# Half of a weight quarter by SyncE's queue in FP32, with a cast on VectorE

## The chip, the core and the metric

The kernel runs on one core of one Trainium2 chip. The metric is the device time of one execution in microseconds (us); the span of a profile is the time from the first to the last instruction of the program inside that execution. The engines go by the profile's names: PE is TensorE (PEld its weight loads), DVE is VectorE, ACT is ScalarE, POOL is GpSimd and SP is SyncE.

## The reference

Attention over 8 batches of 8 heads, 576 tokens and 64 columns per head, with a causal window of 128 tokens and a slope per head on the distance; then a layer norm over the 512 columns of a token and a two-layer perceptron of width 2048, added to its input:

```python
scores = scale * np.matmul(q, k.transpose(0, 1, 3, 2))
mask = (rel >= 0) & (rel < window)
scores = np.where(mask, scores + bias[None], -1000000000.0)
attn = np.exp(scores - np.max(scores, axis=-1, keepdims=True))
x = np.matmul(attn / attn.sum(axis=-1, keepdims=True), v)   # then (B, S, H * D)
xn = (x - mu) / np.sqrt(var + 1e-06) * g_ln
ch = np.maximum(xn @ w_ch1, 0.0) @ w_ch2
return (x + ch).astype(np.float32)
```

All inputs are FP32 in DRAM. The kernel's matmuls take FP16.

## The kernel before, in words

**Tiling.** The 8 x 576 tokens are cut into 36 blocks of 128 tokens (`order`: four pairs of batches, nine blocks each; the ninth holds the 64 last tokens of both batches). A block goes through scores (L500), exponentials on ACT (L511), a mask on DVE (L533), values (L596), the row sums and their reciprocal (L604, L605), and centring (L633, L637). Then it is transposed into `xT` and goes through the perceptron with a group of blocks: the first four groups have two blocks, the other seven have four.

**The weights.** `w1` is the first weight matrix as a tile of 128 partitions x `NKB` = 4 row blocks (`kb`) x 2048 columns in FP16. A quarter of it, c0 to c3, is 512 columns of all four row blocks: 1 MB in DRAM, 512 KB in SBUF. The matmuls of L870 take the 128 columns of one `fb` and go through the four `kb`; c0 serves `fb` 0 to 3, c1 `fb` 4 to 7, and so on. `w1g` is `w1` times the layer norm's gain; `gain_w1` (L226) makes it on DVE from 30 us on. Until then `w1g` is unused. The first two groups use `w1` and have the gain in `xT` (L664, L669, from `g_sb`).

**The loads.** POOL issues nearly all of them, since its queue converts FP32 to FP16 on the way. Their order is the list `loads`: the four loads of `first` (L192: queries and keys of the first block, of batch 0 and then batch 1), values of blocks 0 and 1 (L291), queries and keys of the next blocks (L256, two loads each), c0 of `w1` (L217), values of blocks 2 and 3, c1, c2 and c3 of `w1`, then `w2` by quarters (L236) and further queries, keys and values. POOL's loads have eight semaphores, taken in turn, so the ninth load is issued when the first has landed. SP carries two small loads at the start, the tables (L1288) and the gain `g_sb` (L1289), and next an output at 46 us.

**The order of the work.** Every engine's order is written out by hand: `steps` is a list of groups of calls, and `weave_at` puts them between the matmuls of the perceptron. The steps around the change are these.

- `warm_step(n)`: n matmuls on a tile of ones (L336), which nothing reads.
- `slopes` (L204, DVE, from the tables) and `decay` (L161, ACT); then `add_distances` (L465, PE).
- `turn_first(0)`: the first block of batch 0 is transposed on PE (L416) and copied out of PSUM, queries by DVE (L421) and keys by ACT (L422). Scores follow. The same for batch 1.
- values and centring of those two blocks, `x_step` 0 and 1 (`xT`), the next blocks' queries and keys (`turn_second`, L348, and `copy_second`, L441) and their scores.
- From here on, `mlp1_pair` runs: group 0's `fb` 0 to 11, group 1's `fb` 0 to 7, group 0's 12 to 15, group 1's 8 to 15. Between its first units stand the scores, masks and values of blocks 2 and 3, their transposes (L657) and the steps after them.

Of the kernel before, what the change touches and what calls it, by code (L numbers as in the profile page):

```python
# [11 lines left out]
FP32 = mybir.dt.float32  # L12
# [85 lines left out]
def kernel(  # L98
# [10 lines left out]
    nc = tc.nc  # L109
# [3 lines left out]
    NKB = DM // P  # L113
# [6 lines left out]
    def pool(name, bufs, **kw):  # L120
# [24 lines left out]
    ps_sc = [  # L145
        ps_scores.tile([P, 2, 4 * P], FP32, name=f"ps_sc{i}", tag=f"ps_sc{i}")
        for i in range(2)
    ]
# [24 lines left out]
    w1 = consts.tile([P, NKB, FFN], FP16)  # L173
    w1g = consts.tile([P, NKB, FFN], FP16)
# [37 lines left out]
    w1r = moe_w_ch1.rearrange("(kb p) f -> p kb f", p=P)  # L212
    w2r = moe_w_ch2.rearrange("(fb p) d -> p fb d", p=P)
    W1C = FFN // 4

    def load_w1(c):
        nc.gpsimd.dma_start(  # L217
            out=w1[:, :, c * W1C : (c + 1) * W1C], in_=w1r[:, :, c * W1C : (c + 1) * W1C]
        )

    def gain_w1(first, n):

# [73 lines left out]

    order = [(p, blk) for p in range(NPAIR) for blk in range(NSLOT)]
    w1s, w2s = ([(f, c) for c in range(4)] for f in (load_w1, load_w2))
    weights = {3: w1s[1:] + w2s[:2], 4: w2s[2:], 5: [(load_tables,)]}
    loads, place = [], []  # L300
# [18 lines left out]
    def load_until(n):  # L319
        nonlocal issued  # L320
        while issued < min(n, len(loads)):
            f, *args = loads[issued]
            f(*args)
            issued += 1
# [406 lines left out]
    def scores_step(n):  # L731
        return [(scores,) + order[n]]
# [19 lines left out]
    def warm_step(n):  # L752
        return [[(warm, n)]]
# [1 line left out]

    (low2, high2), (low3, high3) = ([[(attend, *args)] for args in attends(*order[n])] for n in (2, 3))
    steps = warm_step(5) + [[(slopes,), (decay, m_full)]]
    steps += [[(add_distances, ps_sc[b]) for b in range(2)]] + warm_step(1)
    steps += [[(turn_first, 0)], *warm_step(2), scores_step(0)] + warm_step(2)
    steps += [[(turn_first, 1)], *warm_step(2), scores_step(1)]  # L760
    steps += [[(values_at_once, 0, 0, 0), (centre, 0, 0)]] + warm_step(3)
# [27 lines left out]
    for n in range(8, ONE_GO):  # L789
# [14 lines left out]
        for tag, m in (("q", n + 5), ("k", n + 6)):  # L804
            if m < count and order[m][1] % 2 == 0 and by_dma(*order[m]):
                p, blk = order[m]
# [8 lines left out]
    for n in range(ONE_GO, count):  # L815
# [12 lines left out]
        for tag, m in (("q", n + 5), ("k", n + 6)):  # L828
            if m < count and order[m][1] % 2 == 0:
                p, blk = order[m]  # L830
# [455 lines left out]

    def start():
        nc.sync.dma_start(out=first_tables, in_=tables_dram[:, 0 : 3 * P])  # L1288
        nc.sync.dma_start(out=g_sb, in_=moe_g_ln.rearrange("(kb p) -> p kb", p=P))  # L1289
        load_until(place[7])  # L1290

# [6 lines left out]
    with tc.manual_schedule(engines={engine.PE}):  # L1298
        with tc.manual_schedule(engines={engine.Activation, engine.DVE, engine.SP, engine.Pool}):
            start()  # L1300
            advance_to(first)
            weave_at(mlp1_pair((0, 12), (0, 8), (12, NFB), (8, NFB)), 1, 2, 3, 3, 5, 7, 8, 18, 24, 28)
# [60 lines left out]
```

## Time and profile before

| what | before |
| --- | --- |
| time, median of 3 runs | 306.91 us (303.88 to 308.73) |
| the profiled execution: time | 304.83 us |
| its span | 303.1 us |
| granted TensorE clock, mean | 0.998 |
| PE busy | 292.4 us (96%) |
| DVE busy | 232.9 us (77%) |
| ACT busy | 184.6 us (61%) |
| POOL busy | 113.4 us (37%) |
| software DMA queue (POOL's) | 103792 packets, 18.46 MB |
| hardware DMA queue | 45840 packets, 18.60 MB |

The last row counts outputs and transposes besides the two small loads. "Busy" of PE counts pipelined matmuls with modelled ends. A DMA share above 1 in a window means that packets overlap on a DMA engine; the GB/s beside it are of bytes written.

### The profile page before, as it was taken

What the parts mean: (1) busy time and instruction counts of PE and PEld (TensorE: products, weight loads), DVE (VectorE), ACT (ScalarE), POOL (GpSimd) and SP (SyncE); (2) the same over time, 40 slices, a digit from 0 to 9 for tenths busy, and PEclk for the clock granted to TensorE, in tenths of its full rate; (3) what the DMA queues carried; (4) which work ended last, traced back from release to release, by engine and by line L of the source; (5) the groups of instructions that cost most, each with busy time, mean ns of one, the idle gap of its engine ahead of it and who ended that gap; (6) DMA issues with size and microseconds to landing.
All of it is one profiled execution on the core that took longest, in us unless ns stands there. A gap on an engine that the chain in (4) does not pass through costs nothing.

```text
span 303.1 us, 9275 instructions
## 1 busy us (share of the span) xinstructions
PE 292.4 (96%) x3783; PEld 201.0 (66%) x3783; DVE 232.9 (77%) x617; ACT 184.6 (61%) x338; POOL 113.4 (37%) x153
## 2 busy tenths in 40 slices
PE   7679999999999999999999999999999999999994
PEld 2368755866755578656865686568656865788883
DVE  3578678789996788658866886687788878878983
ACT  6578777868967883478457745674577456506500
POOL 8843659683882571684007171760000000000000
PEclk9999999999999999999999999999999999999999
DMA  9999999999999999999979999999561143006014
GB/s 97 170 200 202 193 160 149 202 136 114 147 138 159 171 157 146 148 197 141 123 125 145 151 104 158 139 135 130 108 123 35 21 98 77 19 17 141 3 35 104
DMA packets 150234, 38.03 MB, mean 125 GB/s; under 512 B 140688, under 2 KB 146080, under 8 KB 150192
## 3 DMA queue, kind: packets, MB, share of 16 engines
q0 software_dynamic: 103792, 18.46, 82.7%
q1 hardware_dynamic: 45840, 18.60, 38.8%
q8 instruction: 29, 0.48, 0.7%
q10 hardware_dynamic: 560, 0.39, 0.5%
q14 instruction: 13, 0.11, 0.1%
HBM read 36.90 MB, written 9.44 MB: 153 GB/s over the span
## 4 chain that ended last, share of the span: by engine, by line
PE 88%; DMA 5%; DVE 2%; POOL 1%; ACT 1%; issue 1%; DVEq 0%; POOLq 0%
PE ps_m L870 36%; PE ps_s L1100 22%; PE ps_m L900 9%; PE ps_sc L500 5%; PE ps_sc L596 4%; PE ps_q L1178 4%; DMA w<-in_moe_w_ch_dram 3%; PE ps_x L994 3%; DMA vx<-in_v_dram 2%; POOL first L192 1%; DVE probs L533 1%; PE ps_tx L657 1%; PE ps_pv L567 1%; PE ps_tr L348 1%; PE ps_t L994 1%
## 5 line engine op out<-in xcount | busy, mean ns | idle before, releaser
L870 PE MATMUL ps_m<-xT,w1g 128*128 128x512 f16 (+1 forms) x512 | 104.0, 353 | 0.1
L886 ACT ACTIVATE ht_all<-ps_m 128x512 f16<-128x512 f32 (+1 forms) x143 | 72.0, 511 | 38.6 <-PE ps_m L870 36.6
L870 PEld LDWEIGHTS <-w1g 128*128 128x128 f16 x512 | 47.7, 98 | 41.5 <-issue 0.3
L511 ACT ACTIVATE probs<-ps_sc 128x1024 f16<-128x1024 f32 x56 | 56.1, 1022 | 9.1 <-PE ps_sc L500 9.1
L291 POOL DMA_DIRECT2D vx<-in_v_dram x40 | 35.0, 888 | 67.6 <-PE ps_sc L596 51.5
L1100 PE MATMUL ps_s<-w,s 128*128 128x256 f16 x384 | 45.7, 273 | 0.0
L1100 PEld LDWEIGHTS <-s 128*128 128x128 f16 x384 | 36.8, 98 | 4.3 <-issue 0.2
L533 DVE TENSOR_TENSOR probs<-probs,m 128x1024 f16<-128x1024 f16 x56 | 36.2, 684 | 1.7 <-ACT probs L511 1.7
L1100 PE MATMUL ps_s<-w,ht_all 128*128 128x256 f16 x288 | 36.1, 273 | 0.0
L681 ACT ACTIVATE junk<-xc 128x512 f16<-128x512 f16 x28 | 17.7, 631 | 26.8 <-DVE xc L637 26.8
L900 PE MATMUL ps_m<-w,ht_all 128*128 128x512 f16 x128 | 31.5, 380 | 0.0
L1100 PEld LDWEIGHTS <-ht_all 128*128 128x128 f16 x288 | 27.4, 98 | 4.9
L920 DVE TENSOR_TENSOR s<-ht_all 128x1024 f16<-128x1024 f16 (+2 forms) x36 | 20.5, 569 | 11.3 <-ACT ht_all L886 10.4
L280 POOL DMA_DIRECT2D q<-in_q_dram x40 | 27.6, 711 | 3.1 <-DMA vx<-in_v_dram 1.8
L500 PEld LDWEIGHTS <-k 64*64 64x64 f16 x1088 | 15.5, 107 | 13.5 <-issue 11.6
L605 DVE SCALAR_TENSOR_TENSOR x<-ps_sc,rec 128x512 f16<-128x512 f32 x32 | 22.1, 692 | 1.2 <-DVE rec L604 0.2
L1121 DVE SCALAR_TENSOR_TENSOR o<-ps_s,rstd,x 128x256 f32<-128x256 f32 x48 | 20.9, 477 | 2.6 <-PE ps_s L1100 2.2
L500 PE MATMUL ps_sc<-q,k 64*64 64x128 f16 (+1 forms) x1088 | 21.1, 211 | 1.2 <-ACT k L422 0.6
L277 POOL DMA_DIRECT2D k<-in_k_dram x20 | 17.9, 913 | 6.2 <-DMA k<-k 5.3
L604 DVE RECIPROCAL rec<-ps_sc 128x8 f32<-128x8 f32 x32 | 6.5, 204 | 16.4 <-PE ps_sc L596 16.3
L596 PEld LDWEIGHTS <-probs 128*128 128x128 f16 x384 | 15.9, 98 | 3.6
L900 PEld LDWEIGHTS <-ht_all 128*128 128x128 f16 x128 | 11.0, 98 | 10.6
(116 smaller groups left out, 374.2 us busy)
## 6 DMA issues: line engine op xcount, KB each, us to landing
out_dram<-o SPq DMA_DIRECT2D x64, 128.0 KB, 3.0
vx<-in_v_dram POOLq DMA_DIRECT2D x32, 128.0 KB, 6.6
w<-in_moe_w_ch_dram POOLq DMA_DIRECT2D x8, 512.0 KB, 11.4
k<-in_k_dram POOLq DMA_DIRECT2D x30, 128.0 KB, 7.2
q<-in_q_dram POOLq DMA_DIRECT2D x48, 64.0 KB, 5.8
q<-in_q_dram POOLq DMA_DIRECT2D x10, 128.0 KB, 7.8
out_dram<-o SPq DMA_DIRECT2D x9, 64.0 KB, 2.0
k<-in_k_dram POOLq DMA_DIRECT2D x8, 64.0 KB, 6.5
```

The costliest lines, as they stand in the source:

```text
L280: nc.gpsimd.dma_start(out=t[half, b], in_=tokens.rearrange("h (c r) d -> r c h d", r=2)[r],)
L291: nc.gpsimd.dma_start(out=vx[p0 : p0 + n, :, 0:D], in_=v[b, :, t0 : t0 + n, :].rearrange("h p d -> p h d"),)
L500: nc.tensor.matmul(in_halves(ps[cols, j, n, t, :])[:, r, queries], kt[rows, hp, cols], in_halves(qt[rows, b, hp])[:, r, queries], start=no ...
L511: nc.scalar.activation(out=dst.rearrange("p (n j) q -> p j n q", j=2), in_=ps.rearrange("p j n t q -> p j n (t q)"), func=AF.Exp, scale=in ...
L533: nc.vector.tensor_tensor(out=dst, in0=dst, in1=mask, op=ALU.mult)
L596: nc.tensor.matmul(ps[:, h, 0 : D + 1], pr[:, h, t, :], vext[(p * NSLOT + o) % NV][:, h, :], start=(n == 0), stop=(n == len(terms) - 1),)
L605: nc.vector.scalar_tensor_tensor(out=x.rearrange("p (h d) -> p h d", h=H), in0=ps[:, :, 0:D], scalar=1.0, in1=rec.unsqueeze(2).broadcast_t ...
L870: nc.tensor.matmul(ps[:, 0:cols], w[:, kb, fb * P : (fb + 1) * P], xT[:, kb, 0:cols], start=(kb == 0), stop=(kb == NKB - 1),)
L886: nc.scalar.activation(out=ht[:, fb, :], in_=ps[:, 0:cols], func=AF.Relu)
L900: nc.tensor.matmul(sums[at], ht[:, fb, at * P : (at + 1) * P], w2[:, fb, :], start=(fb == 0), stop=(fb == NFB - 1),)
L1100: nc.tensor.matmul(ps[:, pair, :], lhs[:, fb, at : at + P], rhs[:, fb, :], start=(first and pair == 0 and fb == 0), stop=(fb == half - 1), ...
L1121: nc.vector.scalar_tensor_tensor(out=outs[at][:, cols], in0=ps[:, pair], scalar=rstd[:, n : n + 1], in1=(xs[p, blk] if fresh else outs[at] ...
```

## The change

Of quarter c0, row blocks 0 and 1 no longer come by POOL's queue. SP issues their load, as plain FP32, between its two loads at the start; 512 KB go to the place of `w1g`'s first row block, seen as FP32. DVE casts them into `w1`, in an instruction that stands after `slopes` and before the first copy of `turn_first(0)`. POOL's load of c0 keeps row blocks 2 and 3, at its old place in the order.

```diff
+    by_sync, first_half = slice(0, NKB // 2), w1g[:, 0].bitcast(FP32)
+    first_half = first_half.rearrange("p (kb f) -> p kb f", kb=NKB // 2)
+
     def load_w1(c):
-        nc.gpsimd.dma_start(
-            out=w1[:, :, c * W1C : (c + 1) * W1C], in_=w1r[:, :, c * W1C : (c + 1) * W1C]
-        )
+        kbs, cols = slice(by_sync.stop if c == 0 else 0, NKB), slice(c * W1C, (c + 1) * W1C)
+        nc.gpsimd.dma_start(out=w1[:, kbs, cols], in_=w1r[:, kbs, cols])
+
+    def cast_first_half():
+        nc.vector.tensor_copy(out=w1[:, by_sync, 0:W1C], in_=first_half)
...
-    steps += [[(add_distances, ps_sc[b]) for b in range(2)]] + warm_step(1)
+    steps += [[(add_distances, ps_sc[b]) for b in range(2)] + [(cast_first_half,)]] + warm_step(1)
...
     def start():
         nc.sync.dma_start(out=first_tables, in_=tables_dram[:, 0 : 3 * P])
+        nc.sync.dma_start(out=first_half, in_=w1r[:, by_sync, 0:W1C])
         nc.sync.dma_start(out=g_sb, in_=moe_g_ln.rearrange("(kb p) -> p kb", p=P))
```

## The prediction

> **What bounds the kernel now.** I read the chain of waits first, restricted to the first 24 us, since the change touches nothing later. Its columns are start, length (us) and what was done.
>
> ```profile
> 4.92 6.44 DMA vx<-in_v_dram
> 11.37 0.28 issue
> 11.65 9.84 DMA w<-in_moe_w_ch_dram
> 21.49 0.05 issue
> 21.53 1.05 PE ps_m L870 x8
> ```
>
> The start is bound by the queue of loads: a load of values lands at 11.37, a load of w1 at 21.49, and PE takes up L870 at 21.53. From there to the end the chain is nearly all PE (88% of the whole span), so what is won or lost by about 25 us is carried to the end. Next the waits of PE in the same stretch (us in total, times, longest):
>
> ```profile
> PE ps_tr L348 <- DMA k<-in_k_dram: 1.3, 1, 1.3
> PE ps_m L870 <- DMA w<-in_moe_w_ch_dram: 0.9, 1, 0.9
> PE ps_sc L596 <- DMA vx<-in_v_dram: 0.5, 1, 0.5
> PE ps_tr L416 <- DMA first<-in_k_dram: 0.3, 1, 0.3
> ```
>
> All waits of PE for loads come to 3.0 us; nothing in the change can win more than that. The timeline says where they are (start, length, engine, line, operation, tiles, shape, count, idle time before it):
>
> ```profile
> 3.63 0.49 DVE L204 TENSOR_SCALAR ht_all<-first_tables 128x128 f16<-128x128 f16 x1
> 6.40 0.42 DVE L421 COPY q<-ps_tr 128x512 f16<-128x512 f16 x1 [2.28 <-PE ps_tr L416]
> ...
> 15.32 0.44 PE L348 MATMUL ps_tr<-first_tables,k 64*64 64x64 f16 x30 [1.27 <-DMA k<-in_k_dram]
> 17.27 0.77 PEld L870 LDWEIGHTS <-w 128*128 128x128 f16 x8 [0.23 <-DMA w<-in_moe_w_ch_dram]
> 21.48 0.69 DVE L533 TENSOR_TENSOR probs<-probs,m 128x1024 f16<-128x1024 f16 x1
> 21.53 1.05 PE L870 MATMUL ps_m<-xT,w 128*128 128x256 f16 x8 [0.95 <-DMA w<-in_moe_w_ch_dram]
> 22.42 0.65 PE L596 MATMUL ps_sc<-vx,probs 128*128 128x65 f16 x16
> 24.68 0.23 PEld L657 LDWEIGHTS <-xc 128*128 128x128 f16 x4 [0.29 <-DVE xc L637]
> ```
>
> L870 begins when c0 is there (17.27), but that wait is hardly one: the scores before it end at 16.57 + 0.64 = 17.21, by their own row of the timeline. The real stall is the 0.95 us before 21.53, for c1. So the change is worth something only by letting c1 land earlier in the same queue.
>
> Last, how full the DMA engines are (window and length, busy time of PE, PEld, DVE, ACT, POOL, clock, DMA share, GB/s written):
>
> ```profile
> 2.00:3.00 1.00, 1.00 (x4) 0.38 (x3) 0.22 (x3) 0.23 (x2) 1.00 (x3) 1.00 0.52 84
> 3.00:6.00 3.00, 2.75 (x17) 0.80 (x19) 1.12 (x7) 2.34 (x8) 3.00 (x5) 1.00 1.32 126
> 6.00:9.00 3.00, 2.68 (x84) 1.25 (x84) 0.76 (x2) 2.04 (x3) 3.00 (x5) 1.00 1.97 148
> ```
>
> They are half empty from 2 to 3 us, at 1.32 from 3 to 6, and at 1.97 when fullest.
>
> **What c1 gains.** Queries and keys of the second block release PE at 15.32, c0 at 17.27; the two are neighbours in the queue, so c0 takes 1.95 us of it. Half of it is 0.98 us, and c1 would land at 21.49 - 0.98 = 20.51. PE's matmuls before the stall end at 21.53 - 0.95 = 20.58, so the stall goes. The quarters behind c1 come earlier by as much.
>
> **Where that stall goes.** PE doesn't get all of the 0.95 us. After the eight matmuls of L870 (8 x 0.11 = 0.88) PE wants the values of block 3 (L596) at about 21.5 instead of 22.42. The second half of their weights is masked by the L533 that runs on DVE from 21.48 to 22.17, and this stands behind DVE's work on block 2, which has nothing to do with c1. So the last eight of the sixteen matmuls start at 22.17 at the earliest, and L596, with 0.33 to 0.45 us for them, ends at about 22.6 instead of 23.07. The reciprocal, x, mean and centring of block 3 follow on DVE, and the transposes at 24.68, which wait for that centring, come 0.45 us earlier. So the gain is 0.45 us with nothing on the other side.
>
> **What the new load costs.** It moves 512 KB as 2 KB rows, 256 of them, through the same 16 DMA engines. No load of this kind is in the trace. The nearest row is w1's and w2's own quarters: two POOL loads that wait for successive quarters are issued at 26.84 and 29.38, thus 2.54 us for 512 rows of 2 KB read, and 1.27 us for 256. Upper bound: the whole 1.27 us is taken from POOL's queue, everything up to the keys at 15.32 comes later by that, and c1 lands 1.27 - 0.98 = 0.29 later. Lower bound: nothing, because the new packets find idle engines. SP's tables take 2.0 us from issue to landing (0.74 to 2.74), so the half, issued at 1.1, should flow from about 2.2; from 2 to 3 us there is 1.4 of 1.97 in share to spare, and from 3 to 6 there is 0.65 x 3 = 1.95. That is more than its need, but the first packets of queries and keys lie in the same microseconds, and their landing paces what follows. I take 0.3, near the lower bound, for the part that meets the queue after 3 us.
>
> A rule of the Trainium skill stands against this choice: DMA: Bandwidth & Descriptors, "Issuing engines are not separate DMA queues", says that transfers started by different engines run on the same 16 DMA engines, and that spreading them saves only issue time. By it the term is the upper bound, 1.27; the share of 0.52 beside 1.97 says that the engines are not full when this load comes.
>
> **The cast.** DVE is idle from 4.12 (the end of L204) to 6.40. Landing of the half: at the earliest 1.1 + 2.0 + 1.27 = 4.4, at the latest, with half of the engines' time, 1.1 + 3.0 (an output of 128 KB by SP takes that) + 2.54 = 6.6; I take 5.0. The cast itself, 1024 FP32 elements per partition, isn't in the trace: below, twice the 284 ns of the fastest row (L1043, 512 FP16 elements in SBUF), 0.57; above, twice L878's 683 ns from FP32, 1.37; I take 0.7, as L533 with 1024 elements. While POOL prepares loads, DVE's short instructions stretch: L204 takes from 175 to 495 ns, so 0.3 more. It ends at about 6.0, inside the gap, and costs nothing. Queued behind it are the copies L421, for which the scores wait. If it landed at 6.6 and took 1.37, L421 would end at 8.4 instead of 6.82, and the scores of the first block would begin at 8.4 instead of 7.22; PE's 0.5 us wait for values and its 1.27 us wait for keys at 15.32 take up 1.2 of it, nearly all. So the cover is wide; without it the cost would be that 1.2.
>
> The Trainium skill warns of the cast too: SBUF — State Buffer, "SBUF: two separate sides", says that an FP32 copy of SBUF on VectorE locks GpSimd out of a shared port, so that it can't write descriptors. The stretched L204 agrees that the two meet. POOL would lose one cast; its values issued at 4.92 land at 11.37, far behind their issue, so the sum stays.
>
> **The smaller parts.** `g_sb`, moved behind the half in SP's queue, landed at 1.16 + 2.8 = 3.96 and is first used at 12.39 (L669); even 3 us later costs nothing, and its cover is those 8 us. SP issues nothing else before 46 us. POOL's c0 load has half the rows and needs no longer than before. DVE's writing of `w1g` begins at 30 us, long after the cast.
>
> **The sum.** The gain of 0.45 less 0.3 makes 0.15 us: a span of 303.1 - 0.15 = 302.95 and, with the 1.73 us around it, 304.7 against the profiled execution's 304.83. That execution lies 2.1 below the median of the runs shown; on the median, 306.91 - 0.15 = 306.8. About 2% is what a measurement of this kernel can tell from no change, and this is far inside.
>
> **Rivals.**
>
> 1. The load is hidden wholly: the lower bound, gain 0.45, 306.5. For it, the idle engines at 2 us; against, the first keys already hold PE up for 0.3 us at 5.9. Chance 0.27.
> 2. Nothing is won since the bytes cross the same engines (the rule above): keys 1.27 later, c1 0.29 later. PE then arrives at L596 no earlier in its chain than the gain of 0.45 allows, and the net is 1.27 - 0.45 = 0.82 slower, 307.7. It decides from the point where the delay of the keys passes 0.45. For it, the share of 1.97 right after; against, the 0.52 before. Chance 0.20.
> 3. The cast holds DVE's queue: this needs a landing after about 7.1, beyond the latest estimate. Each us beyond is a us lost; at 9 us, some 2, 308.9. Chance 0.05.
> 4. The change doesn't do what it says: the cast waits not for its own load alone but for the other quarters of w1 that POOL issues earlier in the program, the last landing near 26.6 (POOL goes on at 26.84 after one). DVE would stand until then, the first L421 would come at 27.3 instead of 6.40, and the time would be 306.91 + 20.9 = 327.8. Against it, L870 reads c0 at 17.27 though c1, whose rows lie between c0's, lands at 21.49: waits go by the piece that is read. Chance 0.03.
>
> **How the numbers follow.** The forecast (cost between 0.1 and 0.6) has 0.45, the rivals 0.27, 0.20, 0.05 and 0.03. Faster by over 2% (under 300.8) would need twice all waits of PE for loads; 0.02 for something unseen. Slower by over 2% (over 313) is rival 4 and a large form of rival 3, 0.05. Within 2%: 0.93. The change alone spans -0.45 to +0.82; the runs shown spread from 303.88 to 308.73, and a median of a few can fall anywhere in the middle of that. Hence 304.0 to 309.0.
>
> **What would show it.** Right: the half lands between 4.4 and 6.6, the cast ends before L421's copy is due; PE's wait before the fifth `fb` of L870 is gone; L596 of block 3 waits for DVE's L533; L348's keys come at 15.3 to 15.9. Rival 2 would show in keys at 16.6 and a c1 that isn't earlier; rival 3 in a DVE that waits for the half while PE has ended L416. The prediction is wrong if the span moves by over 1.3 us, or if the first 25 us are unchanged and the time isn't.

## The result and the profile after

The change makes the kernel slower by about 1%: 308.41 us in the median of nine runs (307.33 to 309.43) against 306.34 us for the kernel before (303.50 to 308.73, nine runs). The ratio is 1.0108 with a 95% interval of 1.0078 to 1.0138, so the loss lies between 2.4 and 4.2 us. The ratio counts fast runs only, which leaves out those over 1.5% above the fastest of their kernel (here 308.27 and 308.73 of the kernel before), and so it is larger than the ratio of the two medians. The forecast was 306.8, a gain of 0.15 us; the time fell inside the forecast range and the sign was wrong.

The profiled execution of the changed kernel took 308.41 us with a span of 306.6, against 304.83 and 303.1 before: 3.5 us more of span. Lines of the changed kernel stand six higher than before (L416 is L422, L348 is L354, L870 is L876, L596 is L602).

First its chain of waits over the first 26 us (start, length, what was done), cut at the point where the old chain had a load of w1:

```profile
1.24 0.79 POOL first L192
2.03 6.33 DMA first<-in_k_dram
8.36 0.04 issue
8.40 0.63 PE ps_tr L422 x16
9.03 0.97 PE ps_warm L342 x2
10.00 0.57 PE ps_sc L506 x14
```

The load that ends at 21.49 in the old chain is gone from this one. In its place stands the very first load of keys, which lands at 8.36, and from there on the chain is PE, DVE and ACT. So the front of the chain moved from the queue's tail to its head. PE's waits for loads in the same stretch (us in total, times, longest) say the same:

```profile
PE ps_tr L422 <- DMA first<-in_q_dram: 2.4, 1, 2.4
PE ps_tr L422 <- DMA first<-in_k_dram: 0.6, 1, 0.6
PE ps_sc L602 <- DVE mean L639: 0.5, 1, 0.5
```

The 1.3 us for the second block's keys and the 0.9 us for c1 have gone, since PE now comes later to both; 2.4 us for the first queries have come. The timeline shows each of them in place (start, length, engine, line, operation, tiles, shape, count, idle time before it):

```profile
6.74 0.98 DVE L225 CAST w<-w1g 128x1024 f16<-128x1024 f32 x1 [3.07 <-DMA w1g<-in_moe_w_ch_dram]
7.59 0.22 PE L422 MATMUL ps_tr<-first_tables,first 64*64 64x64 f16 x2 [2.38 <-DMA first<-in_q_dram]
8.40 0.63 PE L422 MATMUL ps_tr<-first_tables,first 64*64 64x64 f16 x30 [0.59 <-DMA first<-in_k_dram]
9.04 0.43 DVE L427 COPY q<-ps_tr 128x512 f16<-128x512 f16 x1 [1.32 <-PE ps_tr L422]
17.65 0.45 PE L354 MATMUL ps_tr<-first_tables,k 64*64 64x64 f16 x32
23.30 1.04 PE L876 MATMUL ps_m<-xT,w 128*128 128x256 f16 x8
25.11 0.42 PE L602 MATMUL ps_sc<-vx,probs 128*128 128x65 f16 x8 [0.53 <-DVE mean L639]
```

What to see here. The cast ended at 7.72, and DVE was then idle for 1.32 us, so the cast held nothing. The first transposes began at 7.59 instead of 5.46. The second block's keys are transposed at 17.65 instead of 15.32, now without a wait, because the delay ate it. L876 at 23.30 has no wait for c1, and L602 is split, its second half waiting for DVE. Last the DMA engines and the granted clock (window and length, busy time of PE, PEld, DVE, ACT, POOL, clock, DMA share, GB/s written):

```profile
2.00:3.00 1.00, 1.00 (x4) 0.36 (x3) 0.36 (x4) 0.38 (x3) 1.00 (x3) 1.00 0.45 86
3.00:6.00 3.00, 2.20 (x7) 0.64 (x5) 0.68 (x6) 2.20 (x8) 3.00 (x5) 1.00 1.13 197
8.00:14.00 6.00, 5.60 (x108) 2.62 (x109) 0.85 (x2) 2.77 (x4) 4.71 (x7) 0.50 1.99 161
```

From 3 to 6 us the share was lower than before (1.13 instead of 1.32), though more bytes were written (197 GB/s instead of 126). And from 8 to 14 us PE ran at half its clock. Thirty transposes took 0.63 us at 8.40, and 0.44 us in the kernel before.

**Whose packets are served.** The view of the DMA queues for the stretch from 3 to 4 us (queue, packets, MB, share of 16 engines; then the load of batch 1's queries, issued at 2.7, with its time to landing) is the one that decides. Before:

```profile
q0 software_dynamic: 451, 0.11, 117.6%
q1 hardware_dynamic: 96, 0.00, 4.7%
...
first<-in_q_dram POOLq DMA_DIRECT2D x1, 128.0 KB, 4.2
```

After:

```profile
q1 hardware_dynamic: 117, 0.24, 94.2%
...
first<-in_q_dram POOLq DMA_DIRECT2D x1, 128.0 KB, 7.3
```

Not one packet of POOL's queue q0 is served in that microsecond, where 451 were before. The 117 packets of SP's load keep the engines busy for 94.2% of 16 us of engine time, which is 0.129 us each. All 256 of them are 256 x 0.129 / 16 = 2.06 us of every engine, and the first queries and keys of batch 0 land behind most of them: the queries at 7.54 instead of 4.68, the keys at 8.36 instead of 5.88. That is more than 2.06 us later. From 4 to 5 us q0 has 95 packets (625 before) beside 107 of q1, and from 5 to 6 us 385 (432 before) beside 360 of q1, of which 345 are under 512 bytes, the packets of `g_sb`. What those add was not measured by itself.

**The account.** Matmul by matmul, PE of the changed kernel is late against the kernel before by 2.1 us at the first transposes, 2.7 at the first scores, 3.8 at about 13 us (1.1 more, under the slow clock), 2.3 at the second block's keys (the old wait for them is used up), 2.8 when the first units of L876 are through, 1.8 after c1's old stall, and 2.45 after the split L602. The step from 2.81 to 2.45, 0.36 us, has the size of the gain that the change was to bring, but it doesn't show that gain: a PE that is this late finds c1 landed in any case. In load_alone (below), where POOL loads all of c0 and c1 lands at 22.15, later than the 21.49 before, the same step is 3.13 to 2.78. Late in the kernel another 1.2 us is added, 0.65 of them where the scores at 89 us wait for transposed queries:

```profile
PE ps_sc L506 <- DMA q<-q: 0.6, 1, 0.6
```

and 0.37 at 290 us, which the profile of a kernel without SP's load (cast_alone, below) has too.

### The profile page after: what moved, and what is told of

Read it like the earlier page. It is cut to its first block, busy times and chain, and to the rows that moved or that the text cites. A ratio compares the mean times of both kernels' runs of the same rounds, so it can differ in the third digit from the quotient of the medians.

```text
span 306.6 us, 9277 instructions
## 1 busy us (share of the span) xinstructions
PE 294.4 (96%) x3783; PEld 201.9 (66%) x3783; DVE 234.1 (76%) x618; ACT 184.5 (60%) x338; POOL 112.6 (37%) x153
## 4 chain that ended last, share of the span: by engine, by line
PE 84%; DVE 7%; DMA 5%; issue 2%; ACT 1%; POOL 0%; DVEq 0%; ACTq 0%; POOLq 0%
PE ps_m L876 33%; PE ps_s L1106 22%; PE ps_m L906 9%; PE ps_sc L506 5%; PE ps_sc L602 4%; PE ps_q L1184 4%; DMA q<-q 3%; PE ps_x L1000 3%; DMA first<-in_k_dram 2%; DVE probs L539 2%; DVE x L611 1%; PE ps_warm L342 1%; DVE s L926 1%; PE ps_pv L573 1%; PE ps_tx L663 1%
## 5 line engine op out<-in xcount | busy, mean ns | idle before, releaser
L876 PE MATMUL ps_m<-xT,w1g 128*128 128x512 f16 (+1 forms) x512 | 103.9, 353 | 0.2 <-DVE o L1252 0.2
L876 PEld LDWEIGHTS <-w1g 128*128 128x128 f16 x512 | 47.7, 98 | 41.4 <-issue 0.4
L297 POOL DMA_DIRECT2D vx<-in_v_dram x40 | 33.9, 854 | 71.2 <-PE ps_sc L602 59.8
L602 PEld LDWEIGHTS <-probs 128*128 128x128 f16 x384 | 15.9, 98 | 4.3 <-DVE mean L639 0.6
```

The costliest lines, as they stand in the source:

```text
L297: nc.gpsimd.dma_start(out=vx[p0 : p0 + n, :, 0:D], in_=v[b, :, t0 : t0 + n, :].rearrange("h p d -> p h d"),)
L602: nc.tensor.matmul(ps[:, h, 0 : D + 1], pr[:, h, t, :], vext[(p * NSLOT + o) % NV][:, h, :], start=(n == 0), stop=(n == len(terms) - 1),)
L876: nc.tensor.matmul(ps[:, 0:cols], w[:, kb, fb * P : (fb + 1) * P], xT[:, kb, 0:cols], start=(kb == 0), stop=(kb == NKB - 1),)
```

## Experiments

The theory was that SP's load, by going ahead of the first queries and keys, costs what was found above. The rivals were the cast, the slow clock by itself, the moved `g_sb`, and the bytes as such, wherever they stand. Ratios are against runs of the kernel before that were taken beside each version's own. "Late by" is PE's delay against the one profile of before, matmul by matmul. This has a spread of its own: at 25 us cast_alone, before_cold and c1_sooner, which load nothing ahead of the first queries, are late by -0.32, -0.34 and 0.40 us.

**The load without the cast (load_alone).** SP brings the half to its place, POOL loads all of c0, nothing is cast.

```diff
-        kbs, cols = slice(by_sync.stop if c == 0 else 0, NKB), slice(c * W1C, (c + 1) * W1C)
+        kbs, cols = slice(0, NKB), slice(c * W1C, (c + 1) * W1C)
...
-    steps += [[(add_distances, ps_sc[b]) for b in range(2)] + [(cast_first_half,)]] + warm_step(1)
+    steps += [[(add_distances, ps_sc[b]) for b in range(2)]] + warm_step(1)
```

> SP loads the 512 KB as in the changed kernel, but nothing reads them: there is no cast, and POOL loads the whole of c0. Theory A (the load alone does it: its packets hold up POOL's first queries and keys on the shared DMA engines, PE stands still from 5.2 to 7.6 us and its clock falls to 0.5): everything up to the scores of the second block is as in the changed kernel, PE's first transposes at 7.6, the clock at 0.5 from about 7.7 for 6.8 us, and c1 about 1 us later than its 20.9 there, still ahead of PE. Time 3.3 us over before, ratio 1.011. Theory B (the cast does it, by holding VectorE's queue or by locking POOL out while it prepares loads): first transposes at 5.5, ratio 1.000 to 1.001.

Measured: 308.35 us, ratio 1.0085 [1.0046, 1.0124], span 306.6. PE is late by 2.7 us at the first scores, 3.0 at 25 us, 3.6 at the end; in the whole change it was 2.7, 2.5 and 3.6. The clock behaved otherwise: it was low from the start until 14.24 us (one warm matmul at 5.41 took 0.63 us, and 0.38 in the kernel before), where in the changed kernel it rose at 4.30 and fell again at 7.71. The queues from 3 to 4 us and PE's waits in the first 26 us:

```profile
q1 hardware_dynamic: 114, 0.23, 85.7%
...
first<-in_q_dram POOLq DMA_DIRECT2D x1, 128.0 KB, 6.5
```
```profile
PE ps_tr L422 <- DMA first<-in_q_dram: 1.7, 1, 1.7
```

Again q0 has no packet from 3 to 4 us. The load alone makes a loss of this size; the cast is not needed for it.

**The cast without the load (cast_alone).** DVE casts 1024 FP32 elements per partition, read from the tables, into an unused place; SP loads nothing more, POOL all of c0.

```diff
+    def cast_first_half():
+        nc.vector.tensor_copy(
+            out=w1g[:, 0, 0 : 8 * P].rearrange("p (n c) -> p n c", c=P),
+            in_=first_tables[:, P:].bitcast(FP32).unsqueeze(1).broadcast_to([P, 8, P]),
...
-    steps += [[(add_distances, ps_sc[b]) for b in range(2)]] + warm_step(1)
+    steps += [[(add_distances, ps_sc[b]) for b in range(2)] + [(cast_first_half,)]] + warm_step(1)
```

> No load by SP, POOL loads the whole of c0; VectorE casts as many FP32 elements at the same place in its order, but takes them from the tables, repeated, and nothing reads the result. Theory A: the cast runs at about 4.1 for 0.7 to 1.0 us, inside VectorE's idle time; first transposes at 5.5, ratio 1.000. Theory B: a good part of the 3.3 us shows, ratio 1.005 or more.

Measured: 305.80 us, ratio 1.0033 [0.9992, 1.0073], no difference that can be told. At 25 us PE is 0.3 us ahead of the old profile. The first transposes came at 6.55, not at 5.5 as expected; the cast can't be the reason, since the tables had landed late already (3.29 instead of 2.76), ahead of it, and the clock was low until 7.91. The queries landed at 4.53. The cast took 0.68 us, and while it ran the two value loads that POOL prepares took longer (timeline of POOL, first before, then here):

```profile
4.05 1.82 POOL L291 DMA_DIRECT2D vx<-in_v_dram  x2
```
```profile
4.04 2.30 POOL L300 DMA_DIRECT2D vx<-in_v_dram  x2
```

So the cast does hold GpSimd, by 0.48 us, and this reached nothing. The rule of SBUF — State Buffer, "SBUF: two separate sides", of the Trainium skill, which the prediction weighed, agrees with this row, and its weight in the sum, nothing, was right. This profile lost 4.3 us of its own at 124 to 131 us, where L879 waited for a transposition of `xc`; what caused that stall is open.

**The change with PE kept at work (after_warm).** Twelve warm matmuls instead of one stand ahead of the first transposes, so that PE is busy until the queries are there.

```diff
-    steps += [[(add_distances, ps_sc[b]) for b in range(2)] + [(cast_first_half,)]] + warm_step(1)
+    steps += [[(add_distances, ps_sc[b]) for b in range(2)] + [(cast_first_half,)]] + warm_step(12)
```

> The changed kernel with twelve matmuls on ones instead of one behind the distances, so that PE is busy while the first queries and keys are awaited (4.8 to about 7.8 us). Theory A says that the delay has two parts: 2.5 us of landing and, since the clock falls to 0.5, about 1.4 us more until the scores of the second block. With the clock kept at 1.0 the first transposes are as late as before (7.6 to 7.8), the transposes of the second block's keys come at about 16.2 instead of 17.65, and the time is 1.4 to 2 us below the changed kernel's: ratio 1.004 to 1.006. If the clock has no part in it (theory A without a clock), nothing changes: ratio 1.011 and the clock at 1.0.

Measured: 307.83 us, ratio 1.0064 [1.0033, 1.0095], span 305.9. The matmuls that replace the idle time, and the transposes behind them:

```profile
5.33 3.73 PE L342 MATMUL ps_warm<-ones 128*128 128x512 f16 x12
8.99 0.45 PE L422 MATMUL ps_tr<-first_tables,first 64*64 64x64 f16 x32
```

The transposes have their full speed (0.45 us for 32). Twelve were a few too many, since PE comes to the transposes at 8.99 with the keys there at 7.95. Still the delay no longer grows: 3.08 us at the first scores, 3.00 at 13.5 us, 1.53 at the second block's keys, 1.89 at 25 us, against 2.50 there in the whole change. So the slow clock is worth some 0.6 us at 25 us by these two profiles, and the larger part is the late loads. But 0.6 is no more than the spread of such profiles, the queries landed 0.45 us earlier here (7.09), and the intervals of the two ratios overlap; this worth is an estimate and not shown.

**Half of the load (one_block).** SP brings one row block (256 KB), POOL the other three.

```diff
-    by_sync, first_half = slice(0, NKB // 2), w1g[:, 0].bitcast(FP32)
-    first_half = first_half.rearrange("p (kb f) -> p kb f", kb=NKB // 2)
+    by_sync, first_half = slice(0, 1), w1g[:, 0, 0 : 2 * W1C].bitcast(FP32)
+    first_half = first_half.rearrange("p (kb f) -> p kb f", kb=1)
```

> The changed kernel with half the load: SP takes one row block of c0 (256 KB), VectorE casts 512 elements per partition, POOL loads three row blocks. Theory A: the first queries and keys land about 1.2 us later than before instead of 2.5 to 2.9, PE is idle for 1.3 us instead of 2.4 and keeps its clock; the wait of 1.27 us for the second block's keys takes up the delay; c1 is some 0.5 us earlier less what the queue lost. Ratio 0.999 to 1.003. If any load ahead of the first queries costs the same (a fixed price), ratio near 1.010.

Measured: 308.14 us, ratio 1.0085 [1.0048, 1.0123]. The expected 0.999 to 1.003 was too low, and the ratio alone doesn't exclude the 1.010 of a fixed price. But half of the load cost 1.78 us at the first scores where all of it cost 2.71, and the clock fell here too (for 3.4 us instead of 6.8). At 25 us PE is late by 1.64. Then the scores at 89 us add 1.4:

```profile
89.45 0.37 PE L506 MATMUL ps_sc<-q,k 64*64 64x128 f16 x16 [1.39 <-DMA q<-q]
```

So the early loss grows with the bytes, but not in proportion: there is a part that half the bytes don't halve, and `g_sb` behind the load is one candidate that was not tested alone. How much of that late wait belongs to the load and how much to the execution that was profiled isn't settled.

**`g_sb` ahead of the half (gain_first).** SP issues the tables, `g_sb`, then the half.

```diff
         nc.sync.dma_start(out=first_tables, in_=tables_dram[:, 0 : 3 * P])
-        nc.sync.dma_start(out=first_half, in_=w1r[:, by_sync, 0:W1C])
         nc.sync.dma_start(out=g_sb, in_=moe_g_ln.rearrange("(kb p) -> p kb", p=P))
+        nc.sync.dma_start(out=first_half, in_=w1r[:, by_sync, 0:W1C])
```

> The changed kernel with SP's second and third load exchanged: g_sb (512 packets of 4 bytes) before the 512 KB. Theory A (the half's own packets hold up POOL's first loads): the half is issued 0.5 us later, the first queries still land at about 7.3 to 7.8, PE's first transposes are 2.2 to 2.6 us later than before, ratio 1.008 to 1.010. Theory G (g_sb, now behind the half, mixes its many small packets into POOL's first loads): a good part of the delay goes, first queries at 6.5 or earlier, ratio 1.004 or less.

Measured: 309.75 us, ratio 1.0173 [1.0129, 1.0216] from four runs of it. The order of `g_sb` was not the main cause: with it in front the half was issued at 1.71 and landed at 7.95, the first queries landed at 7.73, and the second batch's loads moved back to 10.97 and 11.89. The queues from 3 to 4 us:

```profile
q0 software_dynamic: 248, 0.06, 73.2%
q1 hardware_dynamic: 151, 0.05, 22.5%
```

POOL's packets came ahead of the half here, and its first queries were late all the same. So the loss doesn't hang on the half going first; it is enough that the half's packets lie in the microseconds in which POOL's first loads are served. They now lie over more of these loads, and PE is late by 3.09 us at 25 us instead of 2.50; the intervals of the two ratios just overlap. Whether `g_sb` behind the half has a small part in the changed kernel's delay stays open, since the half moved too.

**The half released later (late).** SP's load waits until DVE has copied the second batch's first queries, and the cast stands after the second `xT`.

```diff
+    def load_first_half():
+        nc.vector.memset(first_half[:, 0, 0:2], 0.0)
+        nc.sync.dma_start(out=first_half, in_=w1r[:, by_sync, 0:W1C])
...
-    steps += [[(turn_first, 1)], *warm_step(2), scores_step(1)]
+    steps += [[(turn_first, 1), (load_first_half,)], *warm_step(2), scores_step(1)]
...
-    steps += warm_step(4) + [x_step(1), [(turn_second,), (copy_second,)]]
+    steps += warm_step(4) + [x_step(1) + [(cast_first_half,)], [(turn_second,), (copy_second,)]]
```

> The same load and cast as in the changed kernel, but SP issues the load only when VectorE has copied the first block's queries of batch 1 (about 9.1 us; VectorE clears two columns of the place, which the load waits for), and the cast stands after the second xT, at about 14.6. Theory A: nothing lies ahead of the first loads, so PE's first transposes come at 5.5 as before and the clock stays at 1.0; the load meets the queries and keys of the second block instead, whose landing at 15.3 becomes 1.3 to 2.5 us later; less the 0.45 us of the stall for c1, the time is 0.9 to 2 us over before, ratio 1.003 to 1.007. If only the bytes count, wherever they lie, the ratio is that of the changed kernel, 1.009 to 1.011.

Measured: 307.64 us, ratio 1.0094 [1.0062, 1.0126]. Up to the second block's keys there is no loss at all: PE is 0.4 us ahead at the first scores and 1.0 ahead at 15.4 (the second block's keys landed at 14.30 here and at 15.28 before). Then it falls to 2.0 behind at 19 us:

```profile
16.59 0.69 DVE L229 CAST w<-w1g 128x1024 f16<-128x1024 f32 x1 [1.98 <-DMA w1g<-in_moe_w_ch_dram]
```
```profile
17.67 0.64 PE L510 MATMUL ps_sc<-q,k 64*64 64x128 f16 x32 [2.57 <-DVE q L451]
```

The half landed at 16.57, DVE stood 1.98 us in front of the cast, and the copies of the second block's queries, queued behind it, came late to PE. Behind that stop of PE the clock was low from 18.70 to 22.12, which is in the 2.0. This is the prediction's third rival, in another place. The run shows that the first loads were the cause of the early delay, and that a cast in DVE's order is dear as soon as it waits.

**The same with the cast behind the copies (late_behind), and the half released one batch earlier (mid_behind).** Ahead of these two the question was whether the bytes cost their time wherever they stand.

```diff
-    steps += warm_step(4) + [x_step(1) + [(cast_first_half,)], [(turn_second,), (copy_second,)]]
+    steps += warm_step(4) + [x_step(1), [(turn_second,), (copy_second,), (cast_first_half,)]]
```

and for mid_behind besides:

```diff
-    steps += [[(turn_first, 0)], *warm_step(2), scores_step(0)] + warm_step(2)
-    steps += [[(turn_first, 1), (load_first_half,)], *warm_step(2), scores_step(1)]
+    steps += [[(turn_first, 0), (load_first_half,)], *warm_step(2), scores_step(0)] + warm_step(2)
+    steps += [[(turn_first, 1)], *warm_step(2), scores_step(1)]
```

> As in the late kernel SyncE's half is released by VectorE after the second batch's first copy, but the cast now stands behind the four copies of the second pair instead of ahead of them. Theory A (what costs is work that is held: in the changed kernel the first queries and keys behind the half, in the late kernel VectorE's copies behind the cast that waits for the half until 16.57 us): first queries by 4.8 us, the transposes at 5.5 us, the copies at 16 to 17.5 us without a wait for the cast, the cast 0.7 us long from about 17.5 us, the mask of the third block some 0.5 us later than before, PE at 25 us late by 0.3 to 0.8 us instead of 1.9, ratio 1.000 to 1.004. Rival (512 KB through SyncE beside GpSimd's loads cost their time wherever they stand): delay at 25 us about 1.9 again, ratio 1.007 to 1.010.

> The same with the half released one batch earlier, after the first batch's copy (issue at about 6.3 us). Theory A: first queries and keys as before (by 4.8 and 6 us); the second batch's loads and the second block's keys now share the engines with the half, so the second batch may land 0 to 1.3 us later and PE may lose up to 1.3 us of which the wait for the second block's keys takes most; the half lands by 13 us, so the cast waits for nothing; delay at 25 us 0.3 to 1.0 us, ratio 1.000 to 1.004. Rival (the load costs its time wherever it stands): 1.007 to 1.010.

Measured, late_behind: 306.82 us, ratio 1.0046 [1.0016, 1.0076]. At 25 us PE is late by 0.30 us, instead of 1.91 with the cast ahead of the copies and 2.50 in the whole change. DVE's cast waits for nothing now. Two waits of PE are left, a new one for the cast itself, which PE meets while it is a us ahead, and the old one for c1:

```profile
17.13 1.05 PE L880 MATMUL ps_m<-xT,w 128*128 128x256 f16 x8 [0.90 <-DVE w L229]
21.83 1.05 PE L880 MATMUL ps_m<-xT,w 128*128 128x256 f16 x8 [1.49 <-DMA w<-in_moe_w_ch_dram]
```

The ratio lies a little above the expected 1.000 to 1.004. The profiled execution lost another 1.8 us at 126 us, at a wait for a transposition of `xc` like that of cast_alone; whether this stall is more frequent here is open. And c1 is no earlier here than in the kernel before, so nothing is won either.

Measured, mid_behind: 308.80 us, ratio 1.0132 [1.0089, 1.0176]; both the theory's 1.004 and the rival's 1.010 were too low for its middle. The half, issued at 6.63, met the values of the second batch, whose load landed at 13.24 instead of 9.87 in late_behind:

```profile
13.29 0.42 PE L606 MATMUL ps_sc<-vx,own 128*128 128x65 f16 x8 [2.00 <-DMA vx<-in_v_dram]
```

Later the clock was low again, from 18.97 to 22.38. The price of the same 512 KB, with the cast at one place, thus goes from almost nothing to 2.7 us at 25 us with what is being loaded when it goes out, and the intervals of the two ratios don't overlap. That excludes a fixed price for the bytes.

**A slow clock without a late load (before_cold).** The kernel before without the six warm matmuls at the start.

```diff
-    steps = warm_step(5) + [[(slopes,), (decay, m_full)]]
-    steps += [[(add_distances, ps_sc[b]) for b in range(2)]] + warm_step(1)
+    steps = [[(slopes,), (decay, m_full)]]
+    steps += [[(add_distances, ps_sc[b]) for b in range(2)]]
```

> The kernel before without the six matmuls on ones ahead of the first transposes: the clock without the load. PE's clock is then 0.5 for the first stretch after 5.5 us too, with the loads landing as before. In the changed kernel 6.8 us at 0.5 took the delay from 2.5 to 3.9 us, 1.4 more. Here those 1.4 us meet the wait of 1.27 us for the second block's keys, which takes them up: ratio 1.000 to 1.002, and the transposes of those keys at 15.3 to 15.6. If the slow clock costs by itself: 1.4 us, ratio 1.005.

Measured: 305.35 us, ratio 1.0023 [0.9990, 1.0056], no difference that can be told; the interval still holds the 1.4 us of the rival. The clock was low until 9.37, and PE was late by 0.77 us at 13.5 us. At the second block's keys it was no longer behind:

```profile
14.60 0.45 PE L348 MATMUL ps_tr<-first_tables,k 64*64 64x64 f16 x32
```

This is not what was expected (15.3 to 15.6 after a wait). PE did not wait for these keys at all; they had landed by 14.60, where in the profile of before they landed at 15.28. PE took them up at 14.49 in cast_alone and at 13.89 in c1_sooner, also without a wait, though the loads up to these keys are the same in all four. So the wait of 1.27 us belongs to the one profile of before, and this run doesn't show that such a wait hides a slow clock.

**c1 earlier in POOL's queue (c1_sooner).** The kernel before, with c1 ahead of the values of block 3.

```diff
-    weights = {3: w1s[1:] + w2s[:2], 4: w2s[2:], 5: [(load_tables,)]}
+    weights = {3: w1s[2:] + w2s[:2], 4: w2s[2:], 5: [(load_tables,)]}
...
+        if n == 3:
+            loads += w1s[1:2]
```

> The kernel before with c1 of w1 ahead of the values of block 3 in POOL's queue: what an earlier c1 is worth by itself. c1 should land at about 20.5 instead of 21.49 and the values of block 3 at about 21.5 instead of 19.2, when PE wants them. The stall of 0.95 us before L870 goes, L596 of block 3 then waits for VectorE's mask until 22.2, and the transposes at 24.68 come 0.45 us earlier: ratio 0.997 to 1.000. If the whole stall is worth its length, 0.95 us, ratio 0.997 or less.

Measured: 305.35 us, ratio 1.0021 [0.9982, 1.0061]. In the profile c1 still held PE up, until 21.61:

```profile
PE ps_m L872 <- DMA w<-in_moe_w_ch_dram: 2.5, 3, 1.6
```

So it says little on the worth of an earlier c1, except that this order doesn't win it. When c1 lands differs by itself, too: at 20.64 in before_cold, 21.16 in cast_alone and 21.49 in before. Of all versions, none was faster than the kernel before.

## Why the prediction was wrong

**The step that failed is the cost of the new load.** The prediction gave it 0.3 us, with 1.27 as the upper bound, from two loads of POOL that follow each other at 2.54 us per 512 rows. Measured, the first queries landed 2.86 us later and the first keys 2.48 later, and PE was 2.5 us late at 25 us. Both ends of the bound were wrong for this place, for two reasons. The price was that of rows in a full queue of POOL; SP's own 2 KB packets took 0.129 us of an engine, and 16 of them on each engine make 2.06 us. And the place was misread. The prediction found room on the engines from 2 to 3 us (a share of 0.52) and from 3 to 6 (1.32), and asked whether the bytes fit. They fit. But the first loads were not served as before beside them: none of POOL's packets was served from 3 to 4 us, and in gain_first, where some were, the queries landed as late. The share says how busy engines are, not how long a load takes beside another. The prediction named the danger ("the first packets of queries and keys lie in the same microseconds, and their landing paces what follows") and priced it at 0.3.

The Trainium skill has the rule that fits this row: DMA: Bandwidth & Descriptors, "Queues, rings and completion order", says that each DMA engine takes the queues in turn, and drains a whole packet of one, some 9 to 17 descriptors, before it goes to the next. 256 rows on 16 engines are 16 descriptors each, and a q0 without a packet from 3 to 4 us agrees with one queue being served for that long. From 4 to 6 us both queues have packets in each microsecond, and no run shows how many descriptors an engine takes at a turn. The rule that the prediction did weigh, on transfers that share the same engines, pointed in the right direction and was set aside on the share of 0.52.

**The cover was read from one profile, and was too small.** The prediction said that PE's wait of 1.27 us for the second block's keys, and one of 0.5 us for values ahead of it, would take up an early delay. At the keys 1.47 were taken (3.81 to 2.34), and 0.56 came back at once, where PE waits for DVE before it transposes the queries. But the prediction had thought of this cover for a cast that comes late, not for the load, and a delay of 3.8 us goes through it. Nor can one count on it: before_cold, cast_alone and c1_sooner have no wait for these keys.

**No term for the clock.** The prediction didn't consider it. PE stood for 2.38 us, the clock halved from 7.71 for 6.83 us, and the delay grew by 1.1 us from the first scores to 13.5 us; with PE kept busy it didn't grow. By after_warm some 0.6 of that is still there at 25 us, which is no more than the spread of the profiles.

**What was right, or can't be told.** c1 landed 0.61 us earlier (20.88 instead of 21.49; predicted 0.98), but it landed at 20.64 in before_cold, whose loads are unchanged, so this needn't be the change's doing. Its stall went, and L602 waited for DVE behind the mask as predicted, but load_alone has both without an earlier c1. So the gain of 0.45 was neither shown nor refuted. The second block's keys landed at 15.62, within the 15.3 to 15.9 that were forecast: 0.34 later than before, as the term of 0.3 had it; with the spread of that landing (13.57 in c1_sooner) this is no proof. `g_sb` landed at 7.71 and nothing waited for it. The half landed at 6.72, just past the latest estimate of 6.6; the cast took 0.98 us, as the 0.7 and the stretch of 0.3 had it, and DVE waited on PE behind it. This was luck in part: the cast ended at 7.72, and in the kernel before the copy L421 is due at 6.40. Had the queries come in time, the cast would have held them by 1.3 us. The casts wait for their own load alone, so the fourth rival is excluded.

**The rivals.** The second, that the bytes cross the same engines, has the mechanism and the sign. Its price of 0.82 us, and its place, the second block's keys 1.27 later, were wrong; the price was paid at the first block, and c1 came no later than in the profile of before. The prediction's own test, that it is wrong if the span moves by over 1.3 us, was met: it moved by 3.5.

**What stays open.** Of the 3.5 us of span, 2.5 are explained up to 25 us. The 0.65 at the scores of 89 us is named but was not tested; in one_block the same wait cost 1.4, and load_alone, after_warm and gain_first lose nothing there. The runs of the kernel before that the ratios count lie between 303.5 and 308.1 us, so a single profile of it is no base for the last half microsecond.

## What to carry to other kernels

A transfer on another queue isn't free because the DMA engines are half idle: ask which transfers come next on the same engines, and if these pace the start, count the whole time of the new packets on one engine against them. Put a bulk load behind the loads that the first instructions wait for, and its cast where everything ahead of it has landed and nothing urgent stands behind it. Before you let a wait absorb a delay, see in more than one profile that the wait is there, and add up all that will lean on it, the slower clock after an idle PE included.

## What the runs showed of the hardware

- 117 packets of 2 KB of the hardware queue kept 16 DMA engines busy for 94.2% of a microsecond, 0.129 us each, while the software queue was served nothing. 512 KB took 5.5 us from issue to landing, and 7.7 in late.
- After a stop of PE of 2.38 us the granted clock was halved for 6.83 us, twice the 3.41 us that it stayed low in one_block. TensorE: Matmul & The Clock Gate, "What's actually happening", of the Trainium skill, puts the slow clock after an idle window of about 3.4 us; the stop of 2.38 us behind which it came here was a us shorter than that. In mid_behind the clock fell at 18.97 though PE was busy for 1.89 of the 3.41 us ahead of that and no stop in them was longer than 0.90.
- A cast of 128x1024 FP32 elements took 0.68 us in cast_alone, where POOL's preparation of two loads beside it took 2.30 instead of 1.82 us, and 0.98 us in the changed kernel.
